# The products of zeros at the start of a retention and two-layer FFN kernel: from float32 passes of 64 columns to float32r passes of 512

## The chip, the cores and the metric

The kernel runs on one core of one Trainium2 chip. The metric is the device time of one execution in microseconds (us); the median of three runs stands for the kernel.

## The reference

The program is a retention layer followed by two feed-forward layers.

```python
# q, k, v: (4, 8, 576, 64); 8 heads, 4 sequences, 2304 tokens in all
scores = scale * q @ k.T                      # per sequence and head
ret = (scores * gamma[h] ** (i - j) * (i >= j)) @ v
x = ret, heads side by side                   # (2304, 512)
h = x @ w_in;   x = (h * sigmoid(h)) @ w_out  # layer 0, 512 -> 2048 -> 512
h = x @ w2_in;  x = (max(h, 0) + alpha * min(h, 0)) @ w2_out   # layer 1
```

The products of zeros that this case is about feed no result. They are there in the kernel before and in the changed one, and only their shape, type and number differ.

## The kernel before, in words

**Retention.** The 2304 tokens are 18 blocks of 128. A block arrives in two loads of 512 KB (`att_load`, L444): q and k, then k and v by token. `att_prep` (L455) scales q and v, on POOL or DVE. `att_half` (L468) is one half of a block: eight products of 64x64 for the scores (`sc`) and, except in the half that ends a sequence, eight for the running state (`total`), in float32, which the trace shows as two matmul instructions each. `att_mask` (L486) multiplies the scores by the mask on DVE, and `att_out` (L492) makes the block's output (`xo`), from which ACT and DVE cut the high part `xhi` and the low part `xlo`. `att_step(n)` (L542) loads and prepares block n + 1, issues its two halves, and puts the output of block n between and behind them. The products of zeros (`warm`, L381) stand behind each half of the first `WARM_BLOCKS` blocks.

**Packs and gates.** There are five buffers of blocks (`PACKS`). A load into one that was used before waits for the products that read the old block. `gate` (L386) copies one column on ACT, so that a block's load also waits for the load two blocks earlier.

**Layers.** A weight tile comes by one load of 512 KB and is split into a high and a low part by ACT, DVE and POOL (`weight`). `h_unit` (L564) multiplies a span of up to 512 tokens by one tile of the first weight, in float32r, 12 matmuls in two units; it leaves its result in tiles of the ring `g`. `y_unit` (L592) multiplies those by the second weight. In the first phase one of the 16 tiles of layer 0 is done for all tokens while the retention runs; the rest of both layers follows when the retention has ended.

**Order.** Nothing is issued as it is written. `Program` records every operation, simulates the engines with its own costs (`cost`, L111) and writes each engine's order (`order`, L166; `issue`, L277). TensorE takes units from two queues, retention and layers, each in its own order. All instructions of the trace therefore have line L280, and operations are told apart by the tiles that they write and read. In `cost` a product with a float32r operand is (columns + 32) / 2.4 ns, another one with 128 partitions 110 ns.

**The start.** `zero` (L379) is 192 columns of the first tile of the ring `act`. POOL fills it with zeros (L669), 36 products of zeros are issued, and then `att_step(-1)` begins block 0. The first six blocks are recorded before the first `h_unit` (`LEAD = 4` blocks ahead of the first span of two).

Of the kernel before, what the change touches and what calls it, by code (L numbers as in the profile page):

```python
# [18 lines left out]
P = 128  # L19
# [7 lines left out]
C = 64  # L27
# [2 lines left out]

SIZES = [[1, 2, 3, 4, 4, 2], [4, 4, 4, 4]]
GROUPS = [(i, range(sum(sizes[:n]), sum(sizes[:n + 1]))) for i, sizes in enumerate(SIZES) for n in range(len(sizes))]
WARM, WARM_BLOCKS = 36, 2
DUE = {0: -1e5, 1: 6e3}
LATER = [5, 6, 8, 9, 11, 12]
LEAD = 4
# [247 lines left out]
def retention_ffn_kernel(ctx: ExitStack, tc: tile.TileContext, qkv, w1, w2, alpha, small, out):  # L284
# [9 lines left out]
    nc = Program(tc.nc)  # L294
# [18 lines left out]
    class Ring:  # L313
# [7 lines left out]
        def next(self):  # L321
            self.n += 1
            return self.tiles[(self.n - 1) % len(self.tiles)]

    rings = {k: Ring() for k in ("w0", "w1", "g", "act", "down", "pr", "state", "bank", "raw", "top", "low", "a")}
# [50 lines left out]
        return rings["bank"].next()  # L376


    zero = rings["act"].tiles[0][:, 0:P + C]  # L379

    def warm(n):  # L381
        for _ in range(n):
            nc.tensor.matmul(rings["bank"].tiles[-1][:, 0:C], zero[:, 0:P], zero[:, P:], start=True, stop=True,
                             skip_group_check=True)

    def gate(dst, src):  # L386

# [56 lines left out]
    def att_load(n):  # L444
        if 0 < n < PACKS:
            for i in (0, 2):
                gate(pack(n)[:, i], fac[:, 0] if n == 1 else pack(n - 2)[:, i + 1])
        nc.sync.dma_start(out=pack(n)[:, 0:2], in_=qkv[n, :, 0:2])
        nc.sync.dma_start(out=pack(n)[:, 2:4], in_=qkv[n, :, 2:4])
# [5 lines left out]
    def att_prep(n):  # L455

        prep = ("gpsimd", "tensor_tensor"), ("vector", "tensor_tensor")
        q = pack(n)[:, 0].rearrange("p (c x t) -> p c x t", x=2, t=C)
        at = 2 * n % NCH
        for a, b, x in ((at, at + 2, 0),) if at + 2 <= NCH else ((at, NCH, 0), (0, 1, 1)):  # L460
            if 2 * n < NCH and a:
                att_table(a, b)
            part = q[:, :, x:x + b - a]
            nc.either(prep, out=part, in0=part, in1=qtab[:, :, a:b], op=ALU.mult)
        v = heads(n, 3)
        nc.either(prep, out=v, in0=v, in1=vtab[:, n % PERIOD].unsqueeze(2).to_broadcast([P, H, D]), op=ALU.mult)

    def att_half(n, c):  # L468

        nc.unit("retention", c == 1)  # L470
        q, k = pairs(n, 0), pairs(n, 1)
        j = 1 - c
        g = 2 * n + c
        more = (g + 1) % NCH
        k2, v2 = heads(n, 2)[rows(c)], heads(n, 3)[rows(c)]
        for p in range(NPAIR):
            for i in range(2):
                quarter(two["sc"][rows(i), j, p * C:(p + 1) * C], k[rows(j), p, rows(i)], q[rows(j), p, rows(i)])
                if more:
                    quarter(total[rows(i), p * D:(p + 1) * D], k2[:, 2 * p + i], v2[:, 2 * p + i],  # L480
                            start=g % NCH == 0 and p == 0)
        if more:
            states[g + 1] = rings["state"].next()
            nc.either(COPY, states[g + 1], total[:, 0:NPAIR * D])

    def att_mask(n):  # L486
        probs[n] = rings["pr"].next()
        nc.vector.tensor_tensor(out=probs[n].rearrange("p (j c t) -> p j c t", j=2, c=NPAIR),
                                in0=two["sc"][:, :, 0:NPAIR * C].rearrange("p j (c t) -> p j c t", c=NPAIR),
                                in1=mask, op=ALU.mult)  # L490
# [51 lines left out]
    def att_step(n):  # L542

        m = n + 1
        out = att_out(n) if n >= 0 else iter([None])
        if m < NBLK:
            att_load(m)
            att_prep(m)
            att_half(m, 0)
            if m < WARM_BLOCKS:  # L550
                warm(4)
        next(out)
        if m < NBLK:
            att_half(m, 1)
            if m < WARM_BLOCKS:
                warm(4)
            att_mask(m)
        for _ in out:
            pass
# [100 lines left out]
    def run(*what):  # L660
        for e in what:
            if e == "b":
                for n in blocks:
                    att_step(n)
                    break
            else:
                e()

    nc.gpsimd.memset(zero, 0.0)  # L669
    nc.unit("retention")  # L670
    warm(WARM)
    att_step(-1)
    first = [(s, u) for s in range(len(TILES)) for u in hs[s] + ys[s]]
    at = 0
# [80 lines left out]
```

## Time and profile before

| what | value |
|---|---|
| median of 3 runs | 884.74 us (884.13 to 887.15) |
| the profiled execution's own time | 886.65 us |
| its span, first to last instruction | 884.9 us |
| mean granted TensorE clock over the span | 0.994 |
| TensorE busy | 866.6 us, 98% |
| VectorE busy | 559.7 us, 63% |
| ScalarE busy | 379.6 us, 43% |
| GpSimd busy | 131.0 us, 15% |
| retention ends, layers alone from there | about 107.85 us into the span |

Times within the profile are microseconds from the start of the span. PE is TensorE's matmuls, PEld its weight loads, DVE VectorE, ACT ScalarE, POOL GpSimd. A matmul's end is modelled and matmuls overlap, so the time that one matmul takes in a row of them is read from start to start. A float32 product is two matmul instructions, so 36 products of zeros are 72 rows.

### The profile page before, as it was taken

How to read it: one execution, taken by the hardware profiler on the slowest of the kernel's cores; microseconds unless marked ns; L12 is line 12 of the kernel's file. 1: busy time of each engine (PE TensorE's matmuls, PEld its weight loads, DVE VectorE, ACT ScalarE, POOL GpSimd, SP SyncE). 2: the span in 40 equal slices, each digit the busy share in tenths (PEclk: the TensorE clock that was granted, in tenths of full speed). 3: DMA queues.
4: the chain of work that ended last, by engine and by line, in shares of the span. 5: the costliest groups of instructions: out<-in, count | busy, mean ns of one | idle time of the engine just before them, and what ended most of it. 6: DMA issues, size and time to landing. Idle time of an engine off the chain costs nothing.

```text
span 884.9 us, 14558 instructions
## 1 busy us (share of the span) xinstructions
PE 866.6 (98%) x6036; PEld 731.4 (83%) x6036; DVE 559.7 (63%) x882; ACT 379.6 (43%) x719; POOL 131.0 (15%) x99
## 2 busy tenths in 40 slices
PE   9888999999999999999999999999999999999998
PEld 9776788888888888888888888888888888888887
DVE  3368779984943399636898722894359733954342
ACT  2245564543432255323456444764345533633340
POOL 3256312120210022101110100230003200200000
PEclk9989999999999999999999999999999999999999
DMA  5767132220300022101120000220012100101102
GB/s 200 261 243 264 53 121 70 96 72 1 100 21 1 0 96 96 49 1 47 65 79 24 25 1 0 96 96 1 1 41 102 49 1 1 48 1 47 50 25 95
DMA packets 17491, 58.32 MB, mean 66 GB/s; under 512 B 2064, under 2 KB 2448, under 8 KB 17424
## 3 DMA queue, kind: packets, MB, share of 16 engines
q1 hardware_dynamic: 17424, 57.38, 19.0%
q8 instruction: 47, 0.77, 0.3%
q14 instruction: 20, 0.16, 0.1%
HBM read 52.66 MB, written 4.72 MB: 65 GB/s over the span
## 4 chain that ended last, share of the span: by engine, by line
PE 94%; DVE 4%; issue 2%; ACT 0%; POOL 0%; DVEq 0%; ACTq 0%; POOLq 0%
PE bank L280 89%; PE xo L280 2%; PE sc L280 2%; DVE a L280 2%; DVE act L280 1%; PE total L280 1%; DVE xlo L280 0%; DVE att L280 0%; DVE gb L280 0%; DVE top L280 0%; DVE w L280 0%; DVE g L280 0%; DVE sums L280 0%; DVE xhi L280 0%; DVE w1b L280 0%
## 5 line engine op out<-in xcount | busy, mean ns | idle before, releaser
L280 PE MATMUL bank<-xhi,w 128*128 128x512 f32 (+1 forms) x880 | 251.3, 371 | 0.0
L280 PEld LDWEIGHTS bank<-xhi,w 128*128 128x128 f32 x880 | 160.1, 190 | 28.0
L280 POOL TENSOR_TENSOR low<-low,top 128x512 f32<-128x512 f32 x64 | 93.4, 1464 | 594.5 <-DVE top L280 585.5
L280 DVE TENSOR_TENSOR sums<-bank,sums 128x512 f32<-128x512 f32 (+1 forms) x155 | 100.7, 651 | 98.4 <-PE bank L280 96.6
L280 PE MATMUL bank<-xlo,w 128*128 128x512 f32 (+1 forms) x440 | 162.6, 370 | 0.0
L280 ACT ACTIVATE act<-bank 128x512 f32<-128x512 f32 (+1 forms) x160 | 88.3, 552 | 121.4 <-PE bank L280 118.8
L280 PE MATMUL bank<-xhi,w0b 128*128 128x512 f32 (+1 forms) x400 | 113.2, 368 | 0.0
L280 DVE SCALAR_TENSOR_TENSOR act<-down,nalpha_sb,act 128x512 f32<-128x512 f32 (+1 forms) x80 | 58.7, 734 | 85.0 <-ACT act L280 84.1
L280 PEld LDWEIGHTS bank<-xlo,w 128*128 128x128 f32 x440 | 83.5, 190 | 14.0
L280 ACT ACTIVATE down<-bank 128x512 f32<-128x512 f32 (+1 forms) x80 | 44.3, 554 | 106.5 <-PE bank L280 105.4
L280 PEld LDWEIGHTS bank<-xhi,w0b 128*128 128x128 f32 x400 | 72.6, 189 | 12.6
L280 DVE TENSOR_TENSOR act<-bank,act 128x512 f32<-128x512 f32 (+1 forms) x80 | 50.8, 634 | 45.7 <-ACT act L280 45.6
L280 PE MATMUL bank<-xlo,w0b 128*128 128x512 f32 (+1 forms) x200 | 73.6, 368 | 0.0
L280 PE MATMUL bank<-gb,w1b 128*128 128x512 f32 (+1 forms) x292 | 67.1, 363 | 1.0 <-DVE act L280 1.0
L280 DVE TENSOR_TENSOR gb<-act,gb 128x512 fp32r<-128x512 f32 (+1 forms) x79 | 52.1, 662 | 22.9 <-ACT gb L280 22.6
L280 PE MATMUL bank<-g,w 128*128 128x512 f32 (+1 forms) x268 | 64.3, 370 | 0.0
L280 ACT CAST g<-act 128x512 fp32r<-128x512 f32 (+1 forms) x81 | 47.1, 581 | 39.8 <-DVE act L280 39.8
L280 PE MATMUL bank<-w1b,gb 128*128 128x512 f32 (+1 forms) x268 | 61.9, 380 | 0.2 <-DVE gb L280 0.2
L280 ACT CAST gb<-act 128x512 fp32r<-128x512 f32 (+1 forms) x79 | 45.3, 575 | 38.8 <-DVE act L280 38.7
L280 ACT ACTIVATE top<-raw 128x512 f32<-128x512 f32 x64 | 43.1, 674 | 43.5 <-POOL low L280 34.1
L280 PEld LDWEIGHTS bank<-gb,w1b 128*128 128x128 f32 x292 | 50.6, 189 | 9.8 <-DVE act L280 1.2
L280 PEld LDWEIGHTS bank<-w1b,gb 128*128 128x128 f32 x268 | 48.6, 188 | 10.1 <-DVE gb L280 0.6
(75 smaller groups left out, 1228.1 us busy)
## 6 DMA issues: line engine op xcount, KB each, us to landing
raw<-in_w SPq DMA_DIRECT2D x64, 512.0 KB, 3.6
pack<-in_qkv SPq DMA_DIRECT2D x22, 512.0 KB, 5.5
sums<-in_qkv SPq DMA_DIRECT2D x14, 512.0 KB, 4.9
out<-sums SPq DMA_DIRECT2D x17, 256.0 KB, 2.0
out<-sums SPq DMA_DIRECT2D x2, 128.0 KB, 1.7
att<-in_small SPq DMA_DIRECT2D x1, 214.0 KB, 3.8
alpha_sb<-in_alpha SPq DMA_DIRECT2D x1, 8.0 KB, 5.5
```

The lines of the kernel that those rows point to most:

```text
L280: getattr(getattr(self.nc, name), method)(*args, **kwargs)
```

## The change

The tile of zeros becomes the whole first tile of the ring `g`, in float32r: POOL fills a tile of `act` with zeros and ACT copies it. A product of zeros is one float32r pass of 512 columns over a whole bank, in place of a float32 product of 64 columns. There are 22 ahead of the first block in place of 36, and one behind each half of the first six blocks in place of four behind each half of the first two.

```diff
-WARM, WARM_BLOCKS = 36, 2
+WARM, WARM_BLOCKS = 22, 6
...
-    zero = rings["act"].tiles[0][:, 0:P + C]
+    zero = rings["g"].tiles[0]
 
     def warm(n):
         for _ in range(n):
-            nc.tensor.matmul(rings["bank"].tiles[-1][:, 0:C], zero[:, 0:P], zero[:, P:], start=True, stop=True,
-                             skip_group_check=True)
+            nc.tensor.matmul(rings["bank"].tiles[-1], zero[:, 0:P], zero, start=True, stop=True)
...
             att_half(m, 0)
             if m < WARM_BLOCKS:
-                warm(4)
+                warm(1)
         next(out)
         if m < NBLK:
             att_half(m, 1)
             if m < WARM_BLOCKS:
-                warm(4)
+                warm(1)
...
-    nc.gpsimd.memset(zero, 0.0)
+    nc.gpsimd.memset(rings["act"].tiles[0], 0.0)
+    nc.scalar.copy(zero, rings["act"].tiles[0])
     nc.unit("retention")
     warm(WARM)
     att_step(-1)
```

## Rows read from the trace of the kernel before

**Rows 1.** The page, engines: busy us, share of span, instructions.

```profile
PE 866.6 (98%) x6036; PEld 731.4 (83%) x6036; DVE 559.7 (63%) x882; ACT 379.6 (43%) x719; POOL 131.0 (15%) x99
```

**Rows 2.** Stretch until retention ends: length, busy (instructions) by engine, clock, DMA share, GB/s.

```profile
0.00:107.85 107.85, 94.53 (x2368) 81.87 (x2368) 63.99 (x99) 43.38 (x109) 46.32 (x41) 0.95 0.61 209
```

**Rows 3.** Chain of waits that ended last, first 130 us: start, length, what.

```profile
1.04 15.62 PE bank L280 x72
...
20.69 1.90 PE bank L280 x8
...
40.46 2.84 issue
...
62.68 2.74 PE bank L280 x6
...
79.02 1.59 PE bank L280 x6
```

**Rows 4.** Timeline of PE: start, length, operation, count, idle time before it.

```profile
31.21 1.13 PE L280 MATMUL xo<-pack,att 64*64 64x64 f32 x32 [0.36 <-DVE xlo L280]
...
32.65 0.32 PE L280 MATMUL sc<-pack 64*64 64x64 f32 x2
...
32.76 0.32 PE L280 MATMUL sc<-pack 64*64 64x64 f32 x2
...
35.37 0.72 PE L280 MATMUL xo<-pack,att 64*64 64x64 f32 x32
...
43.90 0.32 PE L280 MATMUL sc<-pack 64*64 64x64 f32 x2
...
44.01 0.33 PE L280 MATMUL sc<-pack 64*64 64x64 f32 x2
...
46.56 0.37 PE L280 MATMUL sc<-sums 64*64 64x64 f32 x1
...
49.29 0.22 PE L280 MATMUL sc<-sums 64*64 64x64 f32 x2
...
49.35 0.22 PE L280 MATMUL sc<-sums 64*64 64x64 f32 x2
```

**Rows 5.** Three stretches with their granted clock (columns as in rows 2).

```profile
28.00:36.00 8.00, 7.27 (x218) 6.77 (x218) 4.75 (x10) 2.12 (x7) 1.96 (x2) 1.00 0.74 243
42.80:48.80 6.00, 5.22 (x121) 4.70 (x125) 3.29 (x7) 3.17 (x7) 3.27 (x4) 0.50 0.43 166
64.00:66.00 2.00, 2.00 (x28) 1.25 (x30) 0.50 (x1) 0.54 (x2) 1.40 (x1) 0.50 0.56 225
```

**Rows 6.** Timeline of the other engines, first 17 us (columns as in rows 4).

```profile
0.73 0.26 POOL L280 MEMSET act<- 128x192 f32 x1 [0.29 <-POOLq L744]
...
2.02 0.21 ACT L280 ACTIVATE nalpha_sb<-nalpha_sb 128x16 f32<-128x16 f32 x1
...
7.50 0.61 ACT L280 CAST w<-a 128x512 fp32r<-128x512 f32 x1
7.52 2.72 POOL L280 TENSOR_TENSOR sums<-sums,att 128x512 f32<-128x512 f32 x2 [6.53 <-DMA sums<-in_qkv]
...
11.87 1.27 POOL L280 TENSOR_TENSOR pack<-pack,att 128x512 f32<-128x512 f32 x1
...
13.60 0.68 DVE L280 TENSOR_TENSOR pack<-pack,att 128x512 f32<-128x512 f32 x1
...
15.08 1.04 POOL L280 TENSOR_TENSOR pack<-pack,att 128x512 f32<-128x512 f32 x1 [1.94 <-DMA pack<-in_qkv]
```

**Rows 7.** Waits of PE, first 100 us: total us, times, longest.

```profile
PE xo L280 <- issue: 6.4, 4, 2.8
```

**Rows 8.** The stretch between two PE stalls (columns as in rows 2).

```profile
36.20:40.50 4.30, 3.54 (x128) 3.06 (x127) 2.28 (x4) 1.12 (x3) 1.29 (x1) 1.00 0.88 299
```

**Rows 9.** The page, DMA queues: packets, MB, share of 16 engines.

```profile
q8 instruction: 47, 0.77, 0.3%
```

**Rows 10.** Timeline of ACT: the first cast into a tile of the ring g.

```profile
50.06 0.41 ACT L280 CAST g<-act 128x256 fp32r<-128x256 f32 x1
```

## The prediction

> **What bounds the kernel now.** I read the engines' totals first: PE is busy 866.6 of 884.9 us [rows 1]. Split where the retention ends, the first 107.85 us hold 94.5 of them [rows 2], so the other 777.05 us hold 772.1. Behind the retention PE has 5 us of idle time and nothing in the change touches its work there. What can be won lies in the first 107.85 us: 13.3 us of idle PE, the products of zeros, and the pace of the real ones.
>
> The chain of waits says who sets the pace there: from 1.04 to 16.66 it is nothing but products of zeros, and behind each half of blocks 0 and 1 another 1.90 us of them [rows 3]. They are on the path: 15.62 + 4 x 1.90 = 23.2 us.
>
> The timeline of PE gives the pace. Two neighbouring pairs of score products start 0.11 us apart at 32.65, 0.11 at 43.90 and 0.06 at 49.29 [rows 4]. At 43.90 the granted clock is 0.50, 1.2 GHz [rows 5]. At 32.65 the column says 1.00 [rows 5], but the pace is that of 43.90 to the hundredth. The same 32 output products take 1.13 us at 31.21 and 0.72 at 35.37 [rows 4]. I read this as a PE at 1.2 GHz from the start until about 35.4, with the column at 1.00 because no change was recorded before. So the products of float32 zeros kept PE "busy" without lifting its clock.
>
> **The change, part by part.** I follow one marker, the first half of block 5, which starts at 46.56 [rows 4], and then ask whether what lies behind it keeps the gain.
>
> *The tile of zeros.* The fill took 0.26 us for 192 columns [rows 6], so at most 0.7 for 512, from 0.73 to about 1.4. POOL has nothing else for the next 6 us (6.53 idle, rows 6). The new copy is 0.61 us by the cast of that shape, behind the small activation that ends at 2.23 [rows 6]: zeros are there at about 2.9, in place of 1.0. ACT has nothing else then, so only PE waits.
>
> *22 passes.* A pass of 512 columns costs 2.74 / 6 = 0.46 us at granted clock 0.50 (less the tail of the last, about 0.44) and 1.59 / 6 = 0.27 at 1.00 (less the tail, about 0.22) [rows 3, 5]. All slow they last 9.7 us, to 12.6; all fast 4.8 us, to 7.7. The stretch that began with dense passes at 62.68 was fast again soon after 66.0 [rows 3, 5], so I take some 3.4 us slow (8 passes) and 14 fast (3.1 us): they end at about 9.5. Block 0 itself is scaled by POOL until 7.52 + 2.72 = 10.24 [rows 6]. It starts at 10.4 in place of 16.6: **-6.2** (bounds -4.0 and -6.3).
>
> *The zeros behind the halves.* 4 x 1.90 = 7.6 us go; 12 passes of 0.22 = 2.6 us come (5.3 if slow): **-5.0** (bound -2.3).
>
> *The pace.* Between 16.60 and 35.4 stand 18.8 - 7.6 = 11.2 us, less 0.7 idle (7.27 busy of 8.00 from 28 to 36, rows 5): 10.5 us of real work at 0.11 where 0.06 is possible. At the fast level that is 0.55 of it: **-4.7** (bound 0).
>
> *A new wait.* Block 0's two halves with their passes take 2 x (0.5 + 0.22) = 1.4 us at the fast pace (eight pairs of pairs of 0.06 us each, rows 4), to 11.9. Block 1 is scaled by POOL until 13.14 and by DVE until 14.28 [rows 6]; neither waits for PE. Before, zeros filled this time and the third half began behind those that ended at 22.59 [rows 3]. Now PE stands from 11.9 to 14.4: **+2.5** (bounds +1.5 if passes and halves run slow, +3). Queued behind it are the output of block 0 and all of block 1.
>
> *The clock after that wait.* The nearest row is the stall of 2.84 us at 40.46, after which the granted clock was 0.50 from 42.8 to 48.8 [rows 3, 5]: 5.2 us busy, of which 0.45, 2.3 us, was lost. A wait of 2.5 is near to it, and the stretch with dense passes inside was shorter, 3.4 us: **+1.6** (bounds 0 and 2.3). The Trainium skill, page "TensorE: Matmul & The Clock Gate", section "HAM oscillation — how this bites in real kernels", has the rule that speaks against this change: a TensorE that is left idle between bursts is throttled again and the next burst starts cold. This trace agrees at 40.46; no row shows yet whether the wait for block 1 is long enough.
>
> *Later blocks.* Block 2 is there when POOL can begin on it at 15.08 [rows 6]. Later loads are gated by copies on ACT or by products of PE, both of which now come earlier. DMA is used 0.61 of this phase and DVE 64.0 of 107.85 us [rows 2], so neither becomes the bound if it shrinks by 12 us. I take 0; the bound is the fetch rival below.
>
> *The tile of g.* The first cast into a tile of that ring ran at 50.06 [rows 10]. It now waits for the last zeros behind block 5, whose second half follows its first (46.56, rows 4) by some 3 us. Both move forward together: 0, at worst 1 us, because the products that read the cast come later still.
>
> Sum: -6.2 - 5.0 - 4.7 + 2.5 + 1.6 = **-11.8 us**. The profiled execution took 886.65 us, 1.75 around its span; 886.65 - 11.8 = 874.9. The median of the runs, 884.74, lies 1.9 below it, so I state **873.0 us**.
>
> **Rivals.**
>
> *A, the fast level holds (0.14).* The wait for block 1 costs no clock (-1.6), and the stall of 2.84 at 40.46 does not come back, nor its slow stretch (-2.3; together -5.1). For it: the stall's place hangs on the number of instructions ahead of it, and 70 matmuls go. Against: four such stalls stood in 100 us [rows 7]. -11.8 - 1.6 - 5.1 = -18.5: **866.2**.
>
> *B, the slow level comes back (0.16).* If PE falls after every wait and 14.4 to the marker runs at 1.2 GHz, the way to the marker is this. Before, 22.6 to 46.56 is 24.0 us, less 3.8 of zeros and 0.7 + 0.8 + 2.8 idle [rows 5, 8, 3]: 15.9 of real work, of which 8.3 (22.6 to 35.4) and 3.1 (42.8 to 46.56) were slow already. The other 4.5 become 8.2; 10 passes of 0.44 and some 2 us of waits are added: 14.4 + 11.4 + 8.2 + 4.4 + 2 = 40.4, a gain of 6.2: **878.5**. For it: retention alone needed from 28 to about 35.4 to become fast.
>
> *C, the pace is not the clock's (0.06).* Were the column's 1.00 right from the start, the pace and the slow stretch after the wait would both fall out: -6.2 - 5.0 + 2.5 = -8.7: **876.0**. The Trainium skill, same page, section "What's actually happening", lets the throttle go once TensorE has been busy for a while, and PE was busy from 1.04 on: by that the clock was full long before 16.6, and the sum would be this one. Against it is the equal pace at 32.65 and 43.90 [rows 4].
>
> *D, instruction fetch (0.14), the one on the other side.* PE's stalls "issue" have no releaser. Between two of them lie 128 + 127 instructions [rows 8], and 2 x 6036 instructions [rows 1] over the 47 packets of an instruction queue [rows 9] are 257: PE runs out of a fetched piece while DMA is full (0.88, rows 8). A block of retention is such a piece. If PE goes faster through the same blocks, pieces are asked for closer together and beside denser loads. Some 12 pieces lie between block 2 and the end of the retention. Now they cost about 8 us (6.4 before output products, rows 7, the rest before scores). At a mean stall of 1.65 us they would cost 11.8 more and the gain is gone; if each cost the longest, 2.84, it is 34 - 8 = 26 more: 874.9 + 26 - 1.9, **899**. Against: most pieces show no stall now. I give 0.08 to a mean near 1.65, which is no change, and 0.06 to more.
>
> **How the numbers follow.** The forecast has 0.50, A 0.14, B 0.16, C 0.06, D 0.14. About 0.3%, 2.7 us, can be told from no change, so faster means under 882.1: forecast, A, B and C, 0.86. Within 0.3%: 0.08. Slower: 0.06. The range reaches from A to B and, for some stalls more, a little above B: **866 to 881**. It leaves out D and about a third of A.
>
> **What would show it.** In the changed profile: 22 passes that begin near 2.9, start 0.43 apart and then 0.22; block 0 at 10.4; PE idle from about 12 to 14.4; neighbouring pairs of score products 0.06 apart for most of 15 to 35; block 5's first half at 34 to 35; the retention's end near 96 in place of 107.85, and behind it the same 777 us. The prediction is wrong if the pairs stay at 0.11 (B), if the passes are fast from the first one on (C), or if stalls "issue" in the first 100 us sum to far more than 8 us (D).

## The result and the profile after

The changed kernel takes 879.15 us, the median of 16 runs (876.5 to 882.62), against 887.05 for the kernel before on the same chip. The ratio is 0.9912, with a 95% interval of 0.9897 to 0.9927: a gain of 7.8 us. One of the 16 executions of the kernel before took 2185.59 us and is left out of the ratio. Forecast were 11.8 us, with 873.0 as the time and 866 to 881 as the range. The direction and the range held; a third of the gain that was worked out is missing. (The kernel before took 2.3 us more here than the 884.74 from which 873.0 was worked out, so the gains are compared, not the times.) This section reads where it went.

One profiled execution of the changed kernel (881.32 us) stands for it here, split at the marker (block 5's first half, 38.27) and at the end of the retention (102.49). The columns are those of [rows 2].

```profile
0.00:38.27 38.27, 29.10 (x589) 22.30 (x589) 18.79 (x28) 11.99 (x33) 13.99 (x16) 0.82 0.76 264
38.27:102.49 64.22, 54.33 (x1711) 43.27 (x1710) 46.22 (x72) 32.34 (x78) 30.41 (x25) 0.97 0.58 194
102.49:879.50 777.01, 772.07 (x3669) 649.50 (x3669) 495.73 (x783) 336.36 (x611) 84.81 (x58) 1.00 0.14 46
```

The last stretch is what it was: 777.0 us, PE busy 772.1. The marker came forward from 46.56 [rows 4] to 38.27, by 8.3 us. But from there to the end of the retention it took 61.3 us before and takes 64.2 now: 2.9 us are given back behind the marker, and 5.4 are left in this execution. More than half of the 2.9 are waits of PE without a releaser ("issue"). Waits of PE from the marker to the end of the retention, before (first two lines) and now:

```profile
PE xo L280 <- issue: 2.8, 2, 1.5
PE sc L280 <- issue: 1.7, 4, 0.4
...
PE total L280 <- issue: 4.2, 5, 1.5
PE sc L280 <- issue: 2.1, 3, 1.1
```

They sum to 4.5 us before and 6.3 now.

The start, in the timeline of all engines (columns as in [rows 4]):

```profile
0.73 0.53 POOL L280 MEMSET act<- 128x512 f32 x1 [0.29 <-POOLq L744]
...
2.15 0.60 ACT L280 CAST g<-act 128x512 fp32r<-128x512 f32 x1
...
2.80 6.99 PE L280 MATMUL bank<-g 128*128 128x512 f32 x22 [2.80 <-ACT g L280]
...
8.62 2.74 POOL L280 TENSOR_TENSOR sums<-sums,att 128x512 f32<-128x512 f32 x2 [7.36 <-DMA sums<-in_qkv]
...
9.96 0.33 PE L280 MATMUL sc<-sums 64*64 64x64 f32 x2 [0.16 <-POOL sums L280]
...
11.41 0.27 PE L280 MATMUL total<-sums 64*64 64x64 f32 x1 [1.13 <-POOL sums L280]
...
13.07 1.74 DVE L280 TENSOR_TENSOR w<-a,low 128x512 fp32r<-128x512 f32 x1 [1.16 <-POOL low L280]
14.73 0.68 DVE L280 TENSOR_TENSOR pack<-pack,att 128x512 f32<-128x512 f32 x1
15.33 0.68 DVE L280 TENSOR_TENSOR att<-sc,att 128x512 f32<-128x512 f32 x1
...
16.11 0.33 PE L280 MATMUL sc<-pack 64*64 64x64 f32 x1 [2.19 <-issue]
```

Zeros are there at 2.80 and the 22 passes end at 9.79, as forecast (2.9 and 9.5); the passes start 0.43 us apart until 6.38 and 0.23 from then on. Block 0 is scaled a microsecond later than before, because its loads landed at 8.6 in place of 7.5 [rows 6]. Block 1 starts at 16.11, where 14.4 was forecast: 0.1 us behind DVE's mask product of block 0, which reads the score banks that block 1 writes.

The granted clock, in the three stretches of this execution in which its record has 0.50 (1.2 GHz). The record begins at 6.48, where the passes become faster; the column reads 1.00 ahead of that.

```profile
13.35:20.07 6.72, 4.53 (x99) 3.38 (x99) 3.97 (x6) 1.40 (x5) 2.22 (x3) 0.50 0.89 285
26.98:33.80 6.82, 5.99 (x119) 4.76 (x119) 1.54 (x3) 1.49 (x4) 1.27 (x1) 0.50 0.67 246
74.90:78.10 3.20, 3.20 (x79) 2.45 (x82) 0.69 (x1) 0.98 (x3) 2.00 (x2) 0.50 0.04 13
```

The first began before block 1 did, so the clock that the 22 passes had lifted served the later passes, block 0's two halves and no other real work. The second began in a stall of PE's instruction fetch. These are longer waits in the chain that ended last, from 20 to 60 us (the last is a load of a block, not a stall of PE):

```profile
25.23 2.58 issue
...
47.74 0.73 issue
52.54 1.41 issue
55.13 5.38 DMA pack<-in_qkv
```

PE's instructions between two such ends, in a stretch of 3.76 us:

```profile
21.50:25.26 3.76, 3.56 (x127) 2.69 (x127) 2.83 (x5) 1.58 (x5) 1.97 (x2) 1.00 0.85 291
```

Counted through the trace from 20 us on, eight of the ten waits "issue" stand behind PE's instructions 449, 705, 1729, 1985, 2241, 2497, 3009 and 3777. In the kernel before six of eight stand behind 961, 1217, 2241, 2753, 3009 and 4033. All of these are 193 more than a multiple of 256, whatever PE was doing there: the instructions come in pieces of 256. The other two of either kernel, 0.36 to 0.62 us long, stand elsewhere and have some other cause. In the 14 traces of this case every wait "issue" of more than 0.85 us between 20 us and the end of the retention stands at such an end. The DMA queues of the changed kernel from 22.0 to 25.3 (first line), and from 25.3 to 26.6 (the other two; packets, MB, share of 16 engines):

```profile
q1 hardware_dynamic: 282, 1.03, 91.3%
...
q1 hardware_dynamic: 105, 0.39, 88.6%
q8 instruction: 1, 0.02, 4.6%
```

PE ran out at 25.23. The one packet of instructions that it needed began only then, at 25.39, behind 1.03 MB of loads, and PE went on at 27.81. In the 14 traces one such packet goes with each piece of the retention: from 20 us on it begins between 0.5 us ahead of and 8.2 us behind the last instruction of its piece, and PE needs it at the end of the next. At each of the 107 stalls at such ends PE went on 2.2 to 3.8 us after that packet had begun, in the median 2.4: the packet's arrival is what ends the stall. The loads are what makes it late, as far as traces can tell: where the packet began within 1 us of its piece's last instruction (45 pieces), loads used 0.12 of DMA meanwhile; where it began more than 4 us behind (54 pieces), they used 0.82 and moved 1.5 MB on average. In the layers behind the retention, with a DMA share of 0.14, no packet began more than 0.5 us behind. By the Trainium skill, page "Runtime: NRT & Kernel Launch", section "Instruction fetch mechanics", an engine's instructions are refilled in blocks of 256 by a DMA queue of its own, at a cost that is "mostly hidden". The size agrees with the 193 + 256 n of these traces; the cost does not, as the runs below show.

### The profile page after: what moved, and what is told of

It reads as the page before. It is cut to its first block, busy times and chain, and to the rows that moved or that the text cites. A ratio compares the mean times of both kernels' runs of the same rounds, so it can differ in the third digit from the quotient of the medians.

```text
span 879.5 us, 14420 instructions
## 1 busy us (share of the span) xinstructions
PE 855.5 (97%) x5966; PEld 715.1 (81%) x5966; DVE 560.7 (64%) x882; ACT 380.7 (43%) x720; POOL 129.2 (15%) x99
## 3 DMA queue, kind: packets, MB, share of 16 engines
q1 hardware_dynamic: 17424, 57.38, 19.6%
## 4 chain that ended last, share of the span: by engine, by line
PE 91%; DVE 5%; issue 2%; DMA 1%; POOL 1%; SPq 0%; ACT 0%; POOLq 0%; DVEq 0%; ACTq 0%
PE bank L280 87%; PE xo L280 2%; DVE a L280 2%; PE sc L280 1%; PE total L280 1%; DMA sums<-in_qkv 1%; DVE act L280 1%; DMA pack<-in_qkv 1%; DVE att L280 0%; POOL sums L280 0%; DVE xlo L280 0%; POOL pack L280 0%; DVE top L280 0%; DVE gb L280 0%; DVE w L280 0%
## 5 line engine op out<-in xcount | busy, mean ns | idle before, releaser
L280 DVE TENSOR_TENSOR act<-bank,act 128x512 f32<-128x512 f32 (+1 forms) x80 | 50.8, 635 | 48.5 <-ACT act L280 48.4
L280 ACT ACTIVATE top<-raw 128x512 f32<-128x512 f32 x64 | 43.1, 674 | 41.6 <-POOL low L280 34.1
L280 PEld LDWEIGHTS bank<-w1b,gb 128*128 128x128 f32 x268 | 48.6, 188 | 10.1 <-DVE gb L280 0.6
```

The lines of the kernel that those rows point to most:

```text
L280: getattr(getattr(self.nc, name), method)(*args, **kwargs)
```

## The experiments

The first six and the last three run in the planned order of the changed kernel, engine by engine: only what stands for the products of zeros is replaced when the instructions are issued, and in two of them one DVE instruction is moved. The other three do the same with the kernel before.

```diff
     def issue(self):
         for i in self.order():
             _, name, method, args, kwargs = self.ops[i][:5]
+            if i in self.zeros:
+                self.zero_products(self.zeros.index(i), *args)
+                continue
```

**The changed kernel again.** No edit.

> The changed kernel once more, beside the others of this group, so that they can be read against it on one chip. Expected 0.991 of the kernel before (0.9897 to 0.9927 was measured), and a trace like the first: slow level (1.2 GHz) from about 13 to 20 and once more behind a stall of PE's instruction fetch between blocks 3 and 5.

Measured: 0.9907 (0.9889 to 0.9926), 879.72 us. The clock came in another way in this execution: the 22 passes took 8.19 us, as the record begins at 9.03 and not at 6.48, and the slow stretches were 15.86 to 19.27 and 29.5 to 32.9. So single numbers of the clock's course differ between executions of one kernel.

**No products of zeros.** `zero_products` returns at once.

> All products of zeros are left out; every other instruction stands in the order of the changed kernel on each engine. Theory (the gain comes from what no longer stands ahead of and behind the first halves, and the 22 passes buy nothing because the clock has fallen again at 13.4, ahead of block 1): block 0 at about 10, block 1 at about 16 as in the changed kernel, slow level from the start until 20 to 25, and a time within 0.2% of the changed kernel (0.989 to 0.993 of before): 2.6 to 4 us of passes are saved and as much is lost by a longer slow stretch. Rival 1 (the dense passes at the start are what the gain comes from): slow level until about 35, over 4 us slower than the changed kernel, 0.996 or more. Rival 2 (the clock does not matter here, the passes only take time): 0.987.

Measured: 0.9866 (0.9842 to 0.9891), 875.14 us: below the theory's range, the number of rival 2. Block 0 began at 8.6, block 1 at 14.8. PE's output products in this run, 16 a row (the first is a row of 15):

```profile
17.51 0.68 PE L285 MATMUL xo<-att,sums 64*64 64x64 f32 x15
...
22.83 0.46 PE L285 MATMUL xo<-att,pack 64*64 64x64 f32 x16
```

0.68 is the slow pace, 0.46 the fast one. The record of the clock begins at 19.11: with no product of zeros at all, PE reached the upper level about when the changed kernel got back to it (20.07). The passes bought no clock there that lasted.

**The 22 passes alone.**

```diff
+        if k < WARM:
+            self.nc.tensor.matmul(out, lhsT, rhs, start=True, stop=True)
```

> The 22 passes at the start stay, the 12 behind the halves of blocks 0 to 5 are left out, all else in the order of the changed kernel. Theory: as without any, 0.989 to 0.993, since the fast level that the 22 passes give is lost in the wait for block 1 around 13.5 to 16. If the passes behind the halves carry the clock (rival), the slow stretch after 13 lasts beyond 22 in place of 20, and the time is over 0.995. If the 22 passes carry it, this run is faster than the one without any by 2 us or more.

Measured: 0.9889 (0.987 to 0.9908), at the lower end of the theory's range, and not faster than the run without any: in time, neither the passes at the start nor the others carry the gain. The trace says less. A stretch of this run (columns as in [rows 2]):

```profile
14.40:31.40 17.00, 12.85 (x373) 12.04 (x374) 10.02 (x16) 4.88 (x16) 5.36 (x5) 0.50 0.87 291
```

The clock stood at 0.50 far beyond 22, which was the sign of the rival (the passes behind the halves carry the clock), while the time is not its time. A run below that has these passes shows as long a slow stretch, so whether they hold the clock up stays open.

**Sparse products in the same places.** The shape alone is undone.

```diff
+        if k >= WARM or k < 16:
+            rhs = rhs.bitcast(F32)
+            self.nc.tensor.matmul(out[:, 0:C], rhs[:, 0:P], rhs[:, P:P + C], start=True, stop=True,
+                                  skip_group_check=True)
```

> The shape alone is undone: 16 float32 products of 64 columns at the start (16 x 0.43 = 6.9 us, as long as the 22 passes lasted) and one behind each half of the first six blocks (0.43 us), all else in the order of the changed kernel. Theory (dense passes lift the clock, sparse ones hold it down): the pace of the score products stays at 0.11 us between pairs until 25 or later, PE at the slow level for 5 to 10 us more than in the changed kernel, so 2 to 4.5 us slower: 0.993 to 0.996. Rival (only the number of products and the place count, not their shape): 0.991 to 0.992, as the changed kernel plus 12 x 0.2 us.

Measured: 0.9957 (0.9943 to 0.9971). The number is the theory's, the reason is not shown: in the profiled execution, the fastest of its nine, the pairs were 0.06 apart from the first half at 19.6 on (the record begins at 18.62), so one sparse product behind a half did not hold the clock down. This run also has 44 PE instructions more than the changed kernel, and the later runs show that their number can count; what made it slower stays open.

**The mask of block 0 first.**

```diff
...
+            mask, lo = self.late
+            order.remove(lo)
+            order.insert(order.index(mask) + 1, lo)
...
```

> The changed kernel with one DVE instruction moved: the last operation of the first weight tile (1.74 us) goes behind block 0's mask product instead of ahead of block 1's scaling and that mask. Theory (block 1's first half waits for the mask of block 0, because both use the score banks, and the mask stands behind the weight operation on DVE): block 1 starts about 1.7 us earlier, near 14.3, always 0.1 us behind the end of that mask; time 0.5 to 1.7 us below the changed kernel, 0.988 to 0.990. Rival (block 1 waits for its own loads and scaling): no change in its start, 0.991.

Measured: 0.9918 (0.9895 to 0.9941). The timeline of DVE and PE, as above:

```profile
13.61 0.68 DVE L291 TENSOR_TENSOR att<-sc,att 128x512 f32<-128x512 f32 x1
...
14.39 0.30 PE L291 MATMUL sc<-pack 64*64 64x64 f32 x2 [2.52 <-DVE att L291]
```

The releaser is shown: block 1 starts at 14.39, 0.1 us behind the mask. But the 1.7 us are worth nothing at the end; this execution's marker came at 38.6, against 38.27. Behind block 1 its clock was at 0.50 for longer than in the changed kernel:

```profile
16.20:33.10 16.90, 14.80 (x319) 11.52 (x312) 7.24 (x14) 4.28 (x13) 5.41 (x5) 0.50 0.83 274
```

**No products, mask first.** Both edits.

> All products of zeros left out, and the same DVE instruction moved. Theory: the gains add up, since neither depends on the other: 0.9866 of the run without products, less 0.5 to 1.7 us, so 0.985 to 0.986, the best of all. Rival (what starts earlier is taken back by the instruction fetch and the loads of later blocks): 0.9866.

Measured: 0.9863 (0.9832 to 0.9894), the rival's number.

**The kernel before without its products behind the halves.** `zero_products` issues the first 36 alone.

> The kernel before, in its own order, without its four products of zeros behind each half of blocks 0 and 1; the 36 at the start stay. It measures the second term of the sum by itself. If the 7.6 us are all on the path: 0.9914 or a little less. If later waits take a third back, as the changed kernel suggests: 0.994.

Measured: 1.0058 (1.0036 to 1.0081). Taking out 7.6 us of products that stood on the path made the kernel 5 us *slower*. Waits of PE from 20 to 116 us in this run:

```profile
PE sc L284 <- issue: 8.5, 5, 3.7
PE total L284 <- issue: 6.1, 4, 2.7
...
PE xo L284 <- issue: 1.4, 2, 1.0
```

That is 16.0 us without a releaser, 14.5 of them at the ends of pieces, where the kernel before has 8.1 and 7.3. The marker did come forward, from 46.6 to 41.6; all of it and more was lost behind it. So I formed another theory: what counts is where the ends of the pieces fall. A half is 32 matmuls and as many weight loads, an output 64 and 64; a block of retention is 256 instructions, as a piece is. So the end of a piece falls at nearly the same place in one block after the other (layer units and the shorter halves at the ends of sequences shift it a little), and with it the packet that follows that end, in front of or behind that block's loads.

**The kernel before without its products at the start.** `zero_products` issues those behind the halves alone.

> The kernel before, in its own order, without its 36 products of zeros at the start; the ones behind the halves of blocks 0 and 1 stay. It measures the first term by itself: block 0 starts near 10.3 in place of 16.6. If the 6.2 us are all on the path: 0.993. If the start is bound by the loads of blocks 1 and 2 just behind, half of it is left: 0.996.

Measured: 0.9908 (0.9883 to 0.9933), 8.2 us, more than the term. Leaving out the products ahead of block 0 alone is worth what the whole change is, though the ends of the pieces move too (table below).

**The same number of instructions, no products behind the halves.**

```diff
+        if 3 <= k < WARM:
+            self.nc.tensor.matmul(out, lhsT, rhs, start=True, stop=True, skip_group_check=True)
+        if k == 0:
+            for _ in range(19):
+                at = out[0:C, 0:C]
+                self.nc.tensor.matmul(at, lhsT[0:C, 0:C], lhsT[0:C, C:2 * C], start=True, stop=True, skip_group_check=True)
```

> The run with float32 products at the start alone, once more, but with 52 products in place of 36: 33 as before and 19 small ones of 64x64 ahead of them, so that as many PE instructions stand ahead of block 2 as in the kernel before (208), and none behind the halves. Theory F (PE's instructions come in pieces of 256, a block of retention is 256 instructions, so the place of a piece's end within a block is the same block after block; leaving out 64 instructions put it where the fetch runs into the loads of a block): the stalls fall from 14.5 us back to 7 to 9, and the 7.6 us of products that are gone show: 0.992 to 0.996. Rival G (PE needs the pauses behind the halves, so that loads keep ahead; the number of instructions plays no part): 1.004 to 1.008 as before.

Measured: 0.9967 (0.9951 to 0.9982), at the upper edge of theory F and far from rival G. With 64 idle instructions (products of zeros, counted with their weight loads) put back at the start, the kernel is 8 us faster than the run without them, although its block 0 starts 3.0 us later (19.6). That later start gives the loads more time, so this run alone does not exclude it as the reason; of the next runs, two change the count without it. Waits of PE from 20 to 116 us:

```profile
PE xo L284 <- issue: 6.3, 5, 2.0
PE sc L284 <- issue: 4.1, 6, 1.0
```

**No products, and 64, 144 or 192 idle instructions.** The small products stand ahead of block 0; N is 16, 36 and 48. With 16 and 36 block 1 starts no later than without any (14.58 and 14.69, against 14.80). The 48 last until about 13 and delay it to 16.61.

```diff
+        if k == 0:
+            for _ in range(N):
+                at = out[0:C, 0:C]
+                self.nc.tensor.matmul(at, rhs[0:C, 0:C].bitcast(F32), rhs[0:C, C:2 * C].bitcast(F32),
+                                      start=True, stop=True, skip_group_check=True)
```

> No passes, but 16 small float32 products of 64x64 (64 PE instructions, about 1 to 2 us of work) while PE waits for block 0; all else in the order of the changed kernel. They do nothing but move the ends of the 256-instruction pieces by 64 instructions, to where the changed kernel has them (within 4). Theory F: the stalls stand at the same instruction numbers, 64 instructions earlier in the work, and sum to 7 to 10 us; the time moves from 0.9866 towards the changed kernel, 0.988 to 0.991. Rival G: 0.9866.

> The same with 36 small products (144 instructions): the ends of the pieces fall in a block where they fell in the run with float32 products at the start alone, which had the largest stalls, 14.5 us. Theory F: stalls of 11 to 15 us and a time of 0.993 to 1.000. Rival G: 0.9866.

> The same with 48 small products (192 instructions): the ends of the pieces fall at a place in a block that no run so far has had, 64 instructions ahead of those of the run without any product, counted the other way round. Theory F: the stalls differ again, 5 to 10 us, 0.985 to 0.992; no sign can be said ahead. Rival G: 0.9866.

Measured: 0.9891 (0.9866 to 0.9915), 1.002 (0.9997 to 1.0043) and 0.99 (0.9877 to 0.9923), against 0.9866 with none. The 144 are clear of noise, a little above the range of theory F, and rule out G. The other two lie in F's ranges, but their intervals overlap that of the run with none, and the 192 carry the later start besides. Waits of PE from 20 to 116 us with 144 more (first three lines), and with none (last two):

```profile
PE xo L285 <- issue: 8.9, 5, 3.2
PE sc L285 <- issue: 7.2, 5, 3.4
...
PE total L285 <- issue: 3.6, 2, 2.8
```

```profile
PE xo L285 <- issue: 5.0, 6, 1.4
...
PE sc L285 <- issue: 0.4, 1, 0.4
```

And the mechanism in the run with 144 more: PE's two pieces up to 52.6, the stall in the chain, SP's loads, and the DMA queues from 48.6 to 53.2 (first q1 line, no packet of q8) and from 53.2 to 54.6.

```profile
44.30:52.60 8.30, 7.50 (x254) 6.98 (x254) 3.90 (x6) 3.74 (x11) 2.99 (x3) 0.79 0.63 190
...
52.61 3.38 issue
...
47.30 2.11 SPq L285 DMA_DIRECT2D sums<-in_qkv  x2
51.02 0.33 SPq L285 DMA_DIRECT2D raw<-in_w  x1
52.06 5.07 SPq L285 DMA_DIRECT2D pack<-in_qkv  x2
...
q1 hardware_dynamic: 288, 1.05, 80.1%
...
q1 hardware_dynamic: 87, 0.33, 79.6%
q8 instruction: 1, 0.02, 4.6%
```

A piece ended at 48.4, just behind the issue of a block's two loads at 47.30. The packet for the piece after next began at 53.4, behind more than 1 MB, and PE, which had run out at 52.6, went on at 56.0.

The runs side by side. The third column is the number of PE instructions for products of zeros ahead of block 6; the fourth is the instruction of a 256-instruction round, counted over the real work, at which pieces end (193 less the third, modulo 256); the fifth is the sum of waits "issue" from 20 to 116 us in one profiled execution.

| kernel | order | idle instructions | piece ends at | stalls us | ratio |
|---|---|---|---|---|---|
| before | before | 208 | 241 | 8.1 | 1 |
| start alone | before | 144 | 49 | 16.0 | 1.0058 |
| behind alone | before | 64 | 129 | 10.2 | 0.9908 |
| start alone, same count | before | 208 | 241 | 10.4 | 0.9967 |
| changed | after | 68 | 125 | 9.2 | 0.9912 |
| changed, again | after | 68 | 125 | 8.7 | 0.9907 |
| mask first | after | 68 | 125 | 8.6 | 0.9918 |
| 22 passes alone | after | 44 | 149 | 11.0 | 0.9889 |
| sparse | after | 112 | 81 | 8.9 | 0.9957 |
| none, mask first | after | 0 | 193 | 9.2 | 0.9863 |
| none | after | 0 | 193 | 5.4 | 0.9866 |
| none + 64 | after | 64 | 129 | 9.4 | 0.9891 |
| none + 144 | after | 144 | 49 | 20.1 | 1.002 |
| none + 192 | after | 192 | 1 | 9.3 | 0.99 |

Both kernels whose pieces end at 49 have the long stalls and the long times, in either order. The last four rows do the same real work in the same order and differ by up to 1.5%, 14 us, nearly twice the gain of the change. A stall sum comes from one execution, and for "none + 144" from the slowest of its twelve; "none, mask first" has 9.2 us of them at the ratio of "none" with 5.4. So the ratios carry the argument.

A stall can cost more than its length, where the clock falls behind it. The profiled executions of "none + 144" and "none" are 20.9 us apart: 14.7 us are stalls, and between its first rise and the end of the retention the clock stood at 0.50 for 29 us in the one and 10 in the other.

"None + 64" has its pieces end where the changed kernel has them, within 4 instructions, and no pass: 0.9891 against 0.9907 and 0.9912. With the piece ends held in place, the passes buy nothing that these runs can show.

## Why the prediction was right, and where its working was not

**The path at the start: right, a microsecond too good.** "Block 0 starts at 10.4 in place of 16.6": two matmuls began at 9.96, and it went on in earnest at 11.41, because the loads landed later than before: 5.2 of the 6.2 us. The run that left out only the first 36 products gained 8.2 us, with its pieces ending elsewhere.

**"The zeros behind the halves: -5.0": not refuted, about the right size.** Alone, their removal cost 5 us. With the piece ends held in place it gained 2.9 us with a start that was 3.0 later; if that start is wholly on the path, 5.9 of the 7.6 us.

**"A new wait: +2.5": the size right, the reason wrong.** Block 1 waits for the mask of block 0 and not for its own scaling, and it started 1.7 us later than I had it. I had followed what block 1 reads and not the score banks that it writes. Moving the mask moved block 1's start by just that, and brought nothing at the end.

**"The clock after that wait: +1.6": the size right, the cause in part.** The clock fell at 13.35 and came back at 20.07; 4.53 us of work at the slow level, times 0.45, are 2.0. But it fell 0.6 us before the wait for block 1 began (13.92); what lay ahead was the start of block 0, where PE was busy 0.33 of the 1.61 us from 9.79 to 11.40. In the changed kernel run again it fell at 15.86, behind a wait for block 1 of 2.41 us. The rule of the Trainium skill that was weighed there, from the page "TensorE: Matmul & The Clock Gate", section "HAM oscillation — how this bites in real kernels", is that a TensorE left idle between bursts is throttled again. The fall at 15.86 agrees with it; the fall at 13.35 came too early to show it at the wait that I had named.

**The pace is the clock's: right, against rival C.** The 22 passes took 6.99 us, 0.43 apart and then 0.23, and a score pair was 0.11 us from the next only where the pace of 0.50 held. The record of the clock in the kernel before begins at 35.47, which is the 35.4 that I read from the pace.

**"The pace: -4.7": the clock rose earlier, but not by the passes.** I had counted on dense passes to lift it for good; without any product it rose at 19.11. What kept it down before were, as far as these traces show, the four float32 products behind each half. With them the record begins 18.9 us after block 0 in the kernel before and 19.5 in "behind alone"; without them 9.6 in "start alone", 8.4 in "start alone, same count" and 10.5 in "none". This is one execution each. With only one such product behind a half ("sparse") the clock rose as early as with none. So the forecast came near partly by luck: the gain is that of leaving products out, not that of their new shape. "0.06 apart for most of 15 to 35" was missed too: the clock stood at 0.50 for 11.9 of those 20 us.

**"Later blocks: I take 0": the step that failed.** It left the fetch of instructions to rival D, as a matter of PE's speed, at 0.14. The fetch hangs on where the pieces end, and the change moves that by 140 instructions, as I had noted under A without a price. What it measured: 0.9866 to 1.002 for the same real work. The stall of 2.84 us that the kernel before had at 40.46, with the slow clock behind it, came back as 2.58 us at 25.23. (D's "some 12 pieces" are about 16, by 2 x 2368 instructions [rows 2] over 256, less two ahead of block 2.) In the profiled execution, 5.4 us are left of the 11.8: the marker came 3.5 us later than the sum gives, of which 1.7 are block 1's late start, and behind it 2.9 us were lost, 1.8 of them in stalls. For the medians, 4.0 us short, "none + 64" against "none" (0.9891 against 0.9866) would put some 2 us to the place of the piece ends, but the intervals overlap, so that size stays open.

**A version that beats both.** The changed kernel without any product of zeros: 0.9866, 4.6 us below the changed kernel in the same group of runs. With the mask moved in both, it is 4.1 us below (0.9863 against 0.9918). How much of that is the passes' own time and how much the place of the piece ends is not separated.

## What to carry to other kernels

Before filler work is added to keep an engine's clock up, run the kernel without it: here the first waits for data undid what the filler had bought, and without it real work brought the clock up no later. When an edit changes the number of instructions on a busy engine, a time that moves by a per cent may be the instruction stream's alignment to the loads and not the edit; issue idle instructions to hold the count, or run several counts, before crediting it. When a producer is moved forward, follow the buffers that it writes as well as those that it reads.

## What the runs showed of the hardware that I had not expected

TensorE's instructions arrive in pieces of 256, each as one 16 KB packet (0.77 MB over 47, [rows 9]) that is late when the data loads fill DMA: it began up to 8.2 us behind the last instruction of its piece, PE went on 2.2 to 3.8 us after it had begun, and a stall lasted up to 3.7 us. Sixty-four idle instructions moved one kernel from 1.0058 to 0.9967 (with a start 3.0 us later), and 144 moved another from 0.9866 to 1.002. The record of the granted clock is empty ahead of its first rise: without any filler it reads 1.00 from 14 to 19 us while 15 output products take the 0.68 us of the 1.2 GHz pace.
